# A third tile for loads of float64 weights in the first pass, its sums of weights all beside the gate matmuls, and the next pass's x scaled later

## The chip, the cores and the metric

The program runs on one core of one Trainium2 chip. The metric is the device time of one execution in microseconds (us); lower is better. TensorE (PE in the profile) multiplies, VectorE (DVE) and ScalarE (ACT) do elementwise work, SyncE (SP) issues nearly all DMAs, GpSimd (POOL) does a little at the start.

## What is computed

Attention on float32 inputs, followed by two feed-forward layers whose four weight matrices arrive as float64.

```
scores = cap * tanh((q @ k.T) / sqrt(64) / cap)          # 4 batches, 12 heads, 448 rows
x = softmax(scores) @ v                                  # -> 1792 x 768
h = x @ w_in;   g = h - tanh(h);              x = g @ w_out    # 768 -> 2048 -> 768
h = x @ w_in2;  g = h / (1 + exp(-1.702 h));  x = g @ w_out2
```

## The kernel before, in words

**Passes and stages.** Attention runs for all four batches first. Then two passes follow, each over two batches (896 rows). A pass has four stages: `gemm_in` of layer 0 (16 blocks of weights), `gemm_out` of layer 0 (16 blocks, in two halves of 8), `gemm_in` of layer 1, called the gate stage here (16 blocks), and `gemm_rows_seven`, the last product (seven sub-products of 4 blocks each, with half-size sums of the operands in the place of an eighth product). Every product is made of three float32r matmuls: high part by high part, high by low, low by high. So each block of weights must be split into `wh` (a cast on ACT, L76) and `wl` (a subtraction on DVE, L88). In the first three stages a block is 36 matmuls; in the last one 18, with 6 more in the first two sub-products for rows left over.

**Loads of doubles (first pass only).** A chunk of 768 KB of float64 weights is loaded by `dbl_dma` (L147) to a tile `wd`, of which there are two. `convert` makes float32 of it: ACT scales the upper word into a tile `wr` (`conv_exp`, L164; there are two of these too), DVE shifts and merges (L171, L177, L181). `conv_or` then stores the float32 chunk to DRAM (`single`, 384 KB) and issues the next `dbl_dma`, so that a load into a `wd` tile begins when that tile has been used up. A main chunk also gets its `wh` and `wl`. Besides the chunks that the stage itself needs, 16 chunks of the last stage's weights are converted ahead: the list `beside` (L140) says beside which blocks, 12 of them in `gemm_out` and 4 in the gate stage. `prepare` works two blocks ahead of PE (`LEAD`).

**Sums of weights.** The last stage needs sums of the quarters of its weight matrix. `sums_b` (L360) makes them in 8 pieces: four loads of 192 KB into tiles `gs`, four adds on DVE, four stores of 192 KB to DRAM tiles `t1` to `t4`. It is a generator that `ahead` advances once for each unit of `due`, and `rate` (set in `moe`, L1076) is what each block adds. A piece takes four steps; at a rate of 1.5 the 16 blocks of the gate stage give 24 steps, which is six pieces, and the other two follow at the start of the last stage.

**The next pass's x.** Attention results of batches 2 and 3 lie in DRAM without their softmax division. During the last stage of the first pass, twelve times, `x_load` (L1050) loads x and a row of reciprocals w into tiles tagged `far` and `t` (two of each), and `x_scale` multiplies them on DVE and splits the result (ACT cast, DVE subtraction). This is done at every second block from the first sub-product on, with one x loaded ahead. `rows_out` uses the same tags for output tiles.

**The last stage's right side.** `left` prepares the other operand for the next sub-product, sums of activation tiles (`add`, L306) and their split (`rl`, L88).

**Order.** After attention, a scheduler that has its own estimate of times places the instructions of each engine; each engine and the SP queue then works through its own list in order.

Of the kernel before, what the change touches and what calls it, by code (L numbers as in the profile page):

```python
# [9 lines left out]
F32 = mybir.dt.float32  # L10
F32R = mybir.dt.float32r
U32 = mybir.dt.uint32
# [25 lines left out]
def attention_moe_moe(ctx, tc, q, k, v, cap, w_in1, w_out1, w_in2, w_out2, out):  # L38
# [3 lines left out]
    P = 128  # L42
# [16 lines left out]
    def pool(name, bufs, **kw):  # L59
        return ctx.enter_context(tc.tile_pool(name=name, bufs=bufs, **kw))  # L60
# [76 lines left out]
    early = [0, 1, 2, 4, 6, 8, 10, 12, 14]  # L137
    A0, I0, R0 = KF, 2 * KF, 3 * KF
    KQ = KF // 4
    beside = [A0 + n for n in (2, 3, 4, 5, 6, 7, 10, 11, 12, 13, 14, 15)] + [I0 + n for n in (5, 8, 11, 14)]  # L140
    extra = {i: R0 + n % 4 * KQ + n // 4 for n, i in enumerate(beside)}
    order = early + [n for i in range(R0) if i not in early for n in (i, extra.get(i)) if n is not None]
    width = [(k1 - k0) * n for _, k0, k1, n in chunks]
# [4 lines left out]
    def dbl_dma():  # L148
        if n_dbl[0] < NCH:
            i = order[n_dbl[0]]  # L150
            src, k0, k1, n = chunks[i]
            t = wd_p.tile([P, WC, 2], U32, tag="wd", name="wd")
            for a in range(k0, k1, WG):
                z = min(k1, a + WG)
                nc.sync.dma_start(
                    out=t[:, (a - k0) * n:(z - k0) * n].rearrange("p (k f) w -> p k (f w)", f=n),
                    in_=src[a * P:z * P].rearrange("(k p) f -> p k f", p=P),
                )
            dbls[i] = t[:, :width[i]]
            n_dbl[0] += 1  # L160
# [472 lines left out]


    late = []

    def run_late():
        while late:
            late.pop(0)()
# [15 lines left out]
    def g_cubic(a, f, ps):  # L655
        n = a.stop - a.start
        t = g_p.tile([P, TC], F32, tag="t", name="g_t")[:, :n]
        far = g_p.tile([P, TC], F32, tag="far", name="g_far")[:, :n]
        th = nc.scalar.activation(out=t, in_=ps, func=AF.Tanh)
        df = nc.vector.tensor_tensor(out=far, in0=ps, in1=t, op=ALU.subtract)  # L660

        def rest():
            last = splits.pop(0) if splits else iter(())
            v = g1_p.tile([P, TC], F32, tag="v", name="g_v")[:, :n]
            if plain[0]:
                q = gr[f][:, a]
            else:
                q = g_p.tile([P, TC], F32, tag="q", name="g_q")[:, :n]
            m = g1_p.tile([P, TC], BF16, tag="m", name="g_m")[:, :n]
            nc.scalar.activation(out=v, in_=t, func=AF.Square)  # L670
            next(last, None)
            nc.scalar.activation(out=q, in_=v, func=AF.Square, scale=CUB_S, bias=cub_a)
            nc.scalar.activation(out=m, in_=v, func=AF.Relu, bias=cub_u)
            nc.vector.tensor_tensor(out=t, in0=v, in1=t, op=ALU.mult)
            next(last, None)
            nc.vector.scalar_tensor_tensor(out=q, in0=q, scalar=CUB_C, in1=t, op0=ALU.add, op1=ALU.mult)
            nc.vector.copy_predicated(out=q, mask=m.bitcast(U16), data=far)
            if not plain[0]:
                splits.append(g_split(a, f, q))
            for _ in last:  # L680
                pass
            if plain[0] and f < KH and a.stop == NT:
                right(0, f)

        def rest_behind():
            with tc.issue_after(th.ins), tc.issue_after(df.ins):
                rest()

        late.append(rest_behind)
        if f == KF - 1 and a.stop == NT and not plain[0]:  # L690
            late.append(lambda: list(splits.pop(0)))
# [89 lines left out]
    def gemm_out():  # L781
        for half in range(2):
            ps = [[ps_next("ps_y") for _ in range(3)] for _ in SPANS]
            for j in range(KF // 2):
                i, (wh, wl) = w_next()
                for (a0, a1), bank in zip(SPANS, ps):
                    for e in range(3):
                        c = slice(e * P, (e + 1) * P)
                        seq = [p for kk in range(2) for p in ((wh, gh, kk), (wh, gl, kk))]
                        seq += [(wl, gh, kk) for kk in range(2)]  # L790
                        for m, (w, x, kk) in enumerate(seq):
                            nc.tensor.matmul(  # L792
                                bank[e][:, :a1 - a0], w[:, kk, c], x[2 * j + kk][:, a0:a1],
                                start=(j == 0 and m == 0), stop=(j == KF // 2 - 1 and m == len(seq) - 1),
                            )
                        if e == 0:
                            (beside_it if a0 else ahead)(i)
                        if a0 == 0 and e == 1:
                            run_late()
                    if j == KF // 2 - 1:  # L800
                        for e in range(3):
                            x_out(3 * half + e, slice(a0, a1), bank[e][:, :a1 - a0])

    def gemm_out_seven():
# [1 line left out]
            return [ps_m.tile([P, 512], F32, tag="m", name="ps_y")[:, :S] for _ in range(3)]  # L806

        def temps(*tags):
            return [(g1_p if t == "v" else g_p).tile([P, TC], F32, tag=t, name="part")[:, :S] for t in tags]

        b11, b22 = ([gr[n + e][:, S:] for e in range(3)] for n in (2, 5))
        LO, HI = slice(0, S), slice(S, NT)
# [71 lines left out]
    def gemm_in_seven():  # L884
# [3 lines left out]
            return [(xh[3 * n + e][:, a], xl[3 * n + e][:, a]) for e in range(3)]  # L888

        def temp(tag):  # L890
            return (g1_p if tag == "v" else g_p).tile([P, TC], F32, tag=tag, name="part")[:, :S]

        right_of = {
            "11": part(0, LO), "12": part(1, LO), "s4": part(1, HI), "s1": part(0, HI),
# [47 lines left out]
    def gemm_rows_seven(b0):  # L942
        def three():
            return [ps_m.tile([P, 512], F32, tag="m", name="ps_o")[:, :HW] for _ in range(3)]

        def kept_sum(i):
            return sums[i // 2][:, i % 2 * HW:(i % 2 + 1) * HW]

# [19 lines left out]
        for p, name in enumerate(SEVEN_B):  # L968
            ps = three()
            for j in range(KQ):  # L970
# [19 lines left out]
                        left(SEVEN_B[p + 1], k)  # L990
                if p == 0 and j == 0:
                    run_late()
                if j % 2:
                    continue
                if loaded:
                    x_scale(*loaded.pop())
                if todo:
                    loaded.append((*todo[0], *x_load(b0 + NB, *todo.pop(0))))
            if p == 0 and side:
# [27 lines left out]
                rows_out(b0, 1, 6, rest[1])  # L1027

    def rows_out(b0, half, n, ps, plus=None, two=False):
        pool_n, tag = ((g_p, "q"), (g1_p, "v"), (g_p, "t"), (g_p, "far"))[n % 4]  # L1030
        o = pool_n.tile([P, TC], F32, tag=tag, name="o")[:, :HW]
        if plus is not None:
            nc.vector.scalar_tensor_tensor(
                out=o, in0=ps[:, :HW], scalar=0.5, in1=plus, op0=ALU.mult, op1=ALU.add
# [22 lines left out]
    def x_scale(s, i, x, w):  # L1057
        nc.vector.tensor_tensor(out=x, in0=x, in1=w, op=ALU.mult)
        x_split(s, i, x)

    def moe(b0):
        if b0 + NB == B:
            side.extend((sums_a(), sums_i()))
            rate[0] = 2.25
            yield from gemm_in(0)
            until("a")
            rate[0] = 0.5
            gemm_out_seven()
            until("i")
            gemm_in_seven()  # L1070
        else:
            yield from gemm_in(0)
            gemm_out()
            plain[0] = True
            open_plain()
            side.append(sums_b())  # L1076
            rate[0] = 1.5
            yield from gemm_in(1)
            rate[0] = 2.0
        gemm_rows_seven(b0)  # L1080

    wz = one_p.tile([P, 512], BF16, name="wz")
# [13 lines left out]
    pinned[0] = False  # L1096
    first.close()
    g_p = pool("g", 2)
    g1_p = pool("g1", 1)
    ps_m = pool("ps_m", 6, space=bass.MemoryType.PSUM)  # L1100
    g_stack = ExitStack()
    g_big = g_stack.enter_context(tc.tile_pool(name="g_big", bufs=1))
# [36 lines left out]
```

## Time and profile before

| | us |
|---|---|
| median of 3 runs (1117.69 to 1120.09) | 1120.02 |
| the profiled execution's own time | 1120.72 |
| its span, first to last instruction | 1118.9 |
| PE busy | 1087.7 (97%) |
| DVE busy | 930.9 (83%) |
| ACT busy | 667.7 (60%) |

PE is busy nearly all the time, so what can be gained lies in the few places where it waits. A matmul's record is longer than the step from its start to the next one's, so the time of a stage is judged against the time of the same number of matmuls in a stretch without waits. Sections of the span: attention to 200 us, `gemm_in` of the first pass to 320, `gemm_out` to 448.6, the gate stage to 566.0, the last stage to 685.7, and from there the second pass.

### The profile page before, as it was taken

The page shows a single profiled execution, that of the slowest core. Times are in us where ns is not written, and L with a number is a line of the kernel's source. Part 1 is how long each engine was busy: PE and PEld are TensorE (multiplying, and loading weights), DVE is VectorE, ACT ScalarE, POOL GpSimd, SP SyncE. Part 2 cuts the span into 40 slices and gives each one's busy share as a digit, 9 for nine tenths or more (in the row PEclk, how much of TensorE's full clock was granted, in tenths as well). Part 3 has the DMA queues.
Part 4 walks back from the last instruction along what each step waited for, and adds up shares of the span by engine and source line. Part 5 has one row for each costly group of instructions (what it writes and reads, how often), then busy time and mean ns, then how long its engine had stood idle before and what let it go on. Part 6 is the DMA issues. An engine that isn't in the chain of part 4 may idle for free.

```text
span 1118.9 us, 16125 instructions
## 1 busy us (share of the span) xinstructions
PE 1087.7 (97%) x5579; PEld 888.8 (79%) x5579; DVE 930.9 (83%) x1467; ACT 667.7 (60%) x1022; POOL 59.0 (5%) x56
## 2 busy tenths in 40 slices
PE   9999998999999898999989999999999999999998
PEld 3333332789898787899979898888999999999997
DVE  4788999789996666988799784989999898889674
ACT  6898887899872322544325553776755554455452
POOL 0013344100000000000000000000000000000000
PEclk9999999999999999999999999999999999999999
DMA  6776686454537688899955748888655333333445
GB/s 143 201 205 182 194 241 206 159 198 141 185 121 261 249 258 270 266 303 296 299 181 171 215 145 281 295 292 297 203 171 195 115 99 115 112 106 106 127 133 151
DMA packets 156466, 220.58 MB, mean 197 GB/s; under 512 B 58672, under 2 KB 108640, under 8 KB 156384
## 3 DMA queue, kind: packets, MB, share of 16 engines
q1 hardware_dynamic: 155088, 218.94, 62.0%
q8 instruction: 44, 0.72, 0.3%
q10 hardware_dynamic: 1296, 0.61, 0.2%
q14 instruction: 38, 0.31, 0.1%
HBM read 160.83 MB, written 58.68 MB: 196 GB/s over the span
## 4 chain that ended last, share of the span: by engine, by line
PE 61%; DMA 15%; DVE 13%; ACT 6%; issue 4%; SPq 2%; ACTq 0%; DVEq 0%
PE ps_h L767 16%; PE ps_y L825 9%; PE ps_h L909 9%; PE ps_o L979 9%; PE ps_pv L491 7%; DMA wd<-in_moe_w_out_dram 6%; PE ps_sc L450 5%; DMA wd<-in_moe_w_in_dram 3%; DMA whole<-t 2%; DVE wd L171 2%; DVE wr L181 2%; ACT wr L164 2%; PE ps_o L964 2%; DVE wl L88 2%; DVE gs L306 1%
## 5 line engine op out<-in xcount | busy, mean ns | idle before, releaser
L767 PE MATMUL ps_h<-xh,wh 128*128 128x384 f32 (+1 forms) x576 | 209.6, 364 | 2.8 <-ACT wh L76 1.8
L767 PE MATMUL ps_h<-xl,wh 128*128 128x384 f32 (+1 forms) x576 | 210.4, 365 | 0.7 <-DVE xl L88 0.7
L76 ACT CAST wh<-whole 128x768 fp32r<-128x768 f32 (+1 forms) x124 | 100.9, 813 | 90.7 <-PE ps_h L909 35.7
L88 DVE TENSOR_TENSOR wl<-whole,wh 128x768 fp32r<-128x768 f32 (+1 forms) x124 | 115.2, 930 | 26.7 <-ACT wh L76 25.4
L767 PE MATMUL ps_h<-xh,wl 128*128 128x384 f32 (+1 forms) x576 | 131.1, 362 | 0.0
L979 PE MATMUL ps_o<-wl,rh 128*128 128x384 f32 x336 | 114.3, 340 | 9.3 <-DVE wl L88 9.2
L767 PEld LDWEIGHTS ps_h<-xh,wh 128*128 128x128 f32 x576 | 108.1, 188 | 16.3 <-ACT wh L76 2.1
L767 PEld LDWEIGHTS ps_h<-xl,wh 128*128 128x128 f32 x576 | 108.1, 188 | 13.3 <-DVE xl L88 1.2
L767 PEld LDWEIGHTS ps_h<-xh,wl 128*128 128x128 f32 x576 | 104.6, 188 | 12.5 <-issue 1.4
L979 PE MATMUL ps_o<-wh,rh 128*128 128x384 f32 x336 | 113.2, 337 | 1.2 <-ACT wh L76 1.0
L979 PE MATMUL ps_o<-wh,rl 128*128 128x384 f32 x336 | 112.9, 336 | 0.0
L76 ACT CAST rh<-gr 128x384 fp32r<-128x384 f32 (+1 forms) x141 | 72.8, 527 | 62.3 <-PE ps_y L825 26.7
L164 ACT ACTIVATE wr<-wd 128x768 f32<-128x768 f32 x64 | 57.7, 903 | 71.5 <-DMA wd<-in_moe_w_out_dram 43.8
L171 DVE TENSOR_SCALAR wd<-wd 128x768 uint16<-128x768 uint16 x57 | 59.7, 1048 | 40.3 <-ACT wr L164 40.3
L88 DVE TENSOR_TENSOR rl<-gr,rh 128x384 fp32r<-128x384 f32 (+1 forms) x141 | 80.0, 577 | 7.4 <-ACT rh L76 6.9
L469 ACT ACTIVATE t<-ps_sc,tsc 128x896 f32<-128x896 f32 x72 | 69.9, 1005 | 26.7 <-PE ps_sc L450 26.6
L792 PE MATMUL ps_y<-gh,wh 128*128 128x512 f32 (+1 forms) x192 | 71.0, 370 | 6.9 <-ACT wh L76 6.9
L979 PEld LDWEIGHTS ps_o<-wl,rh 128*128 128x128 f32 x336 | 63.4, 189 | 12.8 <-DVE wl L88 12.8
L471 ACT ACTIVATE t<-t,cpos 128x896 f32<-128x896 f32 x72 | 72.3, 1041 | 0.4
L792 PE MATMUL ps_y<-gl,wh 128*128 128x512 f32 (+1 forms) x192 | 70.3, 366 | 0.0
L450 PE MATMUL ps_sc<-qk 64*128 64x448 f32 x288 | 68.4, 573 | 0.8 <-ACT qk L76 0.6
L491 PE MATMUL ps_pv<-t,rv 128*64 128x448 f32 x288 | 64.0, 550 | 3.9 <-ACT t L469 3.4
(143 smaller groups left out, 2280.9 us busy)
## 6 DMA issues: line engine op xcount, KB each, us to landing
wd<-in_moe_w_in_dram SPq DMA_DIRECT2D x64, 384.0 KB
wd<-in_moe_w_out_dram SPq DMA_DIRECT2D x32, 768.0 KB
whole<-single SPq DMA_DIRECT2D x51, 384.0 KB
single<-wr SPq DMA_DIRECT2D x48, 384.0 KB
whole<-t SPq DMA_DIRECT2D x32, 384.0 KB
pair<-single SPq DMA_DIRECT2D x32, 384.0 KB
s<-pair SPq DMA_DIRECT2D x32, 384.0 KB
whole<-s SPq DMA_DIRECT2D x32, 384.0 KB
```

Of the source, the lines that this page charges most:

```text
L76: pin(nc.scalar.copy(out=dst, in_=src))
L88: pin(nc.vector.tensor_tensor(out=dst, in0=src, in1=hi.bitcast(F32), op=ALU.subtract))
L164: pin(nc.scalar.mul(out=raws[i][:, :width[i]], in_=dbls[i][:, :, 1].bitcast(F32), mul=2.0 ** -112))
L171: pin(nc.vector.tensor_scalar(out=half[:, :, 2], in0=half[:, :, 1], scalar1=F64_LOW, scalar2=None, op0=ALU.mult))
L450: pin(nc.tensor.matmul(ps[:, j, :S], qk[a, kc], qk[a, :S], start=True, stop=True))
L471: ins = pin(nc.scalar.activation(out=tt[g, c], in_=tt[g, c], func=AF.Exp, scale=cpos))
L491: pin(nc.tensor.matmul(ps[a, :S], w, t[:, j], start=(c == 0), stop=(c == KC - 1)))
L767: pin(nc.tensor.matmul(ps, w[:, kk, :], x[kk][:, a], start=(m == 0), stop=(m == len(seq) - 1)))
L792: nc.tensor.matmul(bank[e][:, :a1 - a0], w[:, kk, c], x[2 * j + kk][:, a0:a1], start=(j == 0 and m == 0), stop=(j == KF // 2 - 1 and m == ...
L825: nc.tensor.matmul(ps[e], w[:, kk, c], x, start=(k == 0 and m == 0), stop=(k == KH - 1 and m == 2))
L909: nc.tensor.matmul(ps, w, x, start=(m == 0), stop=(m == len(seq) - 1))
L979: nc.tensor.matmul(ps[n], x[:, t], w[:, kk, :], start=(k == 0 and m == 0), stop=(k == KH - 1 and m == 2),)
```

## The change

Four things are edited.

1. The tiles `q` (two) and `v`, `m` (one each) move from the pools `g` and `g1` to pools of their own that can be closed (`swap_pools`). After the first block of `gemm_out` in the first pass they are closed, one more `wd` tile is opened in their place and one more `dbl_dma` is issued. From then on every third load of doubles goes to the new tile. At the start of `gemm_rows_seven` the tiles are swapped back.
2. The last four chunks converted beside others are moved from gate blocks 5, 8, 11, 14 to gate blocks 3, 5, 7, 9.
3. The rate of `sums_b` in the gate stage is 2.0 and not 1.5.
4. `x_load` and `x_scale` begin in the third sub-product; there are two x loaded ahead and not one; and from the fifth sub-product on they come at every block.

```diff
-    beside = [...] + [I0 + n for n in (5, 8, 11, 14)]
+    beside = [...] + [I0 + n for n in (3, 5, 7, 9)]
@@ dbl_dma
-            t = wd_p.tile([P, WC, 2], U32, tag="wd", name="wd")
+            more = some.get("wd") if n_dbl[0] % 3 == 0 else None
+            t = (more or wd_p).tile([P, WC, 2], U32, tag="wd", name="wd")
@@ beside run_late
+    some = {}
+    def temp_p(tag):
+        return some.get(tag, g_p)
+    def swap_pools(**kinds):
+        if "stack" in some:
+            some.pop("stack").close()
+        some.clear()
+        some["stack"] = ExitStack()
+        for name, bufs in kinds.items():
+            some[name] = some["stack"].enter_context(tc.tile_pool(name=f"some_{name}", bufs=bufs, side="right"))
+    def open_temps():
+        swap_pools(q=2, v=1)
@@ gemm_out
                         if a0 == 0 and e == 1:
                             run_late()
+                            if half == j == 0:
+                                swap_pools(wd=1)
+                                dbl_dma()
@@ gemm_rows_seven
+        if "wd" in some:
+            open_temps()
...
-                if j % 2:
+                if p < 2 or (p + j) % 2 and p < 4:
                     continue
-                if loaded:
-                    x_scale(*loaded.pop())
+                if len(loaded) > 1 or loaded and not todo:
+                    x_scale(*loaded.pop(0))
                 if todo:
                     loaded.append((*todo[0], *x_load(b0 + NB, *todo.pop(0))))
@@ moe
             side.append(sums_b())
-            rate[0] = 1.5
+            rate[0] = 2.0
             yield from gemm_in(1)
-            rate[0] = 2.0
         gemm_rows_seven(b0)
```

No instruction is added or removed on any engine. PE's order is the same. What moves, moves on DVE, ACT and SP between the start of `gemm_out` and the end of the first pass.

At the start of `gemm_out`, on SP. `single` are stores of converted chunks, `wd` the loads of doubles. Before:

```order
L185 DMA single32_218<-wr_3369 128x768
L155 DMA wd_3375<-in_moe2_w_out_dram 128x2x768
L185 DMA single3_189<-wr_3395 128x768
L155 DMA wd_3401<-in_moe_w_out_dram 128x2x768
L185 DMA single36_222<-wr_3425 128x768
```

and now:

```order
L186 DMA single32_218<-wr_3379 128x768
L156 DMA wd_3365<-in_moe2_w_out_dram 128x2x768
L156 DMA wd_3385<-in_moe_w_out_dram 128x2x768
L186 DMA single3_189<-wr_3405 128x768
L156 DMA wd_3411<-in_moe2_w_out_dram 128x2x768
```

One more load is issued there, and every later load stands one store earlier in the queue.

At the entry to the last stage, on DVE: from the `wl` of the stage's first block to that of its second (`whole` is a block loaded from DRAM, `gs` a tile of sums, `gr` a tile of activations, `restl` the low part of left-over rows). Before:

```order
L88 TENSOR_TENSOR wl_5242<-whole_5183,wh_5241 128x768
L699 SCALAR_TENSOR_TENSOR gr13_4248<-g_t_5236,ps_h_5217 128x384
L306 TENSOR_TENSOR gs0_4251<-gr0_4235,gr8_4243 128x384
L88 TENSOR_TENSOR restl13_4302<-gr13_4248,resth13_4301 128x128
L306 TENSOR_TENSOR gs7_4258<-gs7_4258,gs6_4257 128x384
L306 TENSOR_TENSOR gs0_4251<-gs0_4251,gr0_4235 128x384
L306 TENSOR_TENSOR gs6_4257<-gs6_4257,gs4_4255 128x384
L306 TENSOR_TENSOR gs1_4252<-gr1_4236,gr9_4244 128x384
...
L88 TENSOR_TENSOR wl_5294<-whole_5245,wh_5293 128x768
```

and now:

```order
L88 TENSOR_TENSOR wl_5270<-whole_5213,wh_5269 128x768
L715 SCALAR_TENSOR_TENSOR gr13_4258<-g_t_5264,ps_h_5245 128x384
L307 TENSOR_TENSOR gr3_4248<-gr3_4248,gr11_4256 128x384
L88 TENSOR_TENSOR restl13_4312<-gr13_4258,resth13_4311 128x128
...
L88 TENSOR_TENSOR wl_5326<-whole_5273,wh_5325 128x768
```

There were 14 instructions between the two and there are 9. From the first `wl` to the fourth there were 37 besides these and there are 25: adds of the last pieces of sums and x are gone from there, and adds of `left` for later sub-products now stand before the first `wl`.

In the first two sub-products, on SP (`w` and `x` are the next pass's). Before:

```order
L252 DMA whole_5362<-single35_221 128x768
L527 DMA w_5399<-wrow2_112 64x448 x2
L252 DMA whole_5407<-single36_222 128x768
L527 DMA w_5487<-wrow2_112 64x448 x2
L527 DMA w_5583<-wrow2_112 64x448 x2
L1053 DMA x_5582<-xd2_2_100 128x448
L252 DMA whole_5449<-single37_223 128x768
```

and now:

```order
L253 DMA whole_5401<-single35_221 128x768
L253 DMA whole_5437<-single36_222 128x768
L253 DMA whole_5471<-single37_223 128x768
L253 DMA whole_5505<-single38_224 128x768
L253 DMA whole_5545<-single39_225 128x768
```

The loads of x and w now stand among the blocks of the fourth to sixth sub-products (ten of x and all twelve pairs of w there; before, six of x and eight pairs of w stood among those of the fourth and fifth).

## Rows read from the trace of the kernel before

**Rows 1.** What TensorE waited for; columns: us in total, times, longest.

```profile
PE ps_o L979 <- DVE wl L88: 9.2, 9, 3.3
PE ps_y L792 <- ACT wh L76: 6.9, 5, 2.5
```

**Rows 2.** Busy time by stage, 320 to 686 us; (x) counts instructions.

```profile
core 0: us, PE busy (x) PEld busy (x) DVE busy (x) ACT busy (x) POOL busy (x), PEclk, DMA share, GB/s
320.10:382.80 62.70, 59.22 (x291) 52.06 (x289) 43.40 (x60) 22.99 (x32) 0.00 (x0) 1.00 0.66 228
382.80:448.60 65.80, 60.83 (x288) 52.84 (x288) 44.26 (x57) 21.82 (x30) 0.00 (x0) 0.98 0.79 258
448.60:507.00 58.40, 57.42 (x282) 51.13 (x283) 50.68 (x81) 28.70 (x50) 0.00 (x0) 1.00 0.88 285
507.00:566.00 59.00, 59.00 (x295) 53.05 (x294) 46.84 (x77) 22.35 (x40) 0.00 (x0) 1.00 0.93 303
566.00:590.10 24.10, 19.17 (x98) 17.95 (x97) 23.63 (x49) 8.78 (x18) 0.00 (x0) 0.93 0.49 151
590.10:624.60 34.50, 34.50 (x200) 34.33 (x199) 29.05 (x53) 18.46 (x35) 0.00 (x0) 1.00 0.59 176
624.60:656.80 32.20, 28.59 (x158) 26.84 (x157) 27.70 (x48) 18.41 (x33) 0.00 (x0) 1.00 0.64 194
656.80:685.70 28.90, 27.45 (x153) 26.04 (x151) 18.10 (x31) 10.44 (x17) 0.00 (x0) 1.00 0.61 184
```

**Rows 3.** Chain of work, second pass: start us, us, what.

```profile
685.95 116.50 PE ps_h L767 x576
...
1059.86 12.48 PE ps_o L979 x72
```

**Rows 4.** Chain of work in the first half of gemm_out.

```profile
342.61 1.04 DVE wd L171
...
345.48 4.97 DMA wd<-in_moe_w_out_dram
...
369.51 1.04 DVE wd L171
...
372.37 6.28 DMA wd<-in_moe_w_out_dram
```

**Rows 5.** What ScalarE waited for, 322 to 450 us.

```profile
ACT wr L164 <- DMA wd<-in_moe_w_out_dram: 41.6, 17, 3.9
```

**Rows 6.** TensorE in order of time: first stall of gemm_out, its cause in brackets.

```profile
372.90 0.50 PE L792 MATMUL ps_y<-gh,wh 128*128 128x512 f32 x1 [1.22 <-ACT wh L76]
```

**Rows 7.** DMA issues of the whole run.

```profile
wd<-in_moe_w_out_dram SPq DMA_DIRECT2D x32, 768.0 KB
...
single<-wr SPq DMA_DIRECT2D x48, 384.0 KB
...
gs<-single SPq DMA_DIRECT2D x32, 192.0 KB
```

**Rows 8.** Chain of work in the gate stage: a store of a chunk.

```profile
546.28 4.17 DMA single<-wr
```

**Rows 9.** VectorE in order of time at the entry to the last stage.

```profile
565.19 0.95 DVE L88 TENSOR_TENSOR wl<-whole,wh 128x768 fp32r<-128x768 f32 x1
...
572.56 0.56 DVE L306 TENSOR_TENSOR gs<-gs,gr 128x384 f32<-128x384 f32 x1
573.03 0.95 DVE L88 TENSOR_TENSOR wl<-whole,wh 128x768 fp32r<-128x768 f32 x1
573.90 0.55 DVE L699 SCALAR_TENSOR_TENSOR gr<-g_t,ps_h 128x384 f32<-128x384 f32 x1
...
585.26 0.96 DVE L88 TENSOR_TENSOR wl<-whole,wh 128x768 fp32r<-128x768 f32 x1
```

**Rows 10.** What the SP queue waited for, 566 to 686 us.

```profile
SPq L252 <- DVE wl L88: 43.5, 26, 3.7
SPq L1053 <- DVE xl L88: 7.5, 7, 2.3
```

More of the change, by code (lines that the diff above doesn't have):

```diff
@@ L139, in attention_moe_moe @@
     KQ = KF // 4
-    beside = [A0 + n for n in (2, 3, 4, 5, 6, 7, 10, 11, 12, 13, 14, 15)] + [I0 + n for n in (5, 8, 11, 14)]
+    beside = [A0 + n for n in (2, 3, 4, 5, 6, 7, 10, 11, 12, 13, 14, 15)] + [I0 + n for n in (3, 5, 7, 9)]
     extra = {i: R0 + n % 4 * KQ + n // 4 for n, i in enumerate(beside)}
@@ L663, in rest @@
             last = splits.pop(0) if splits else iter(())
-            v = g1_p.tile([P, TC], F32, tag="v", name="g_v")[:, :n]
+            v = temp_p("v").tile([P, TC], F32, tag="v", name="g_v")[:, :n]
             if plain[0]:
@@ L667, in rest @@
             else:
-                q = g_p.tile([P, TC], F32, tag="q", name="g_q")[:, :n]
-            m = g1_p.tile([P, TC], BF16, tag="m", name="g_m")[:, :n]
+                q = temp_p("q").tile([P, TC], F32, tag="q", name="g_q")[:, :n]
+            m = temp_p("v").tile([P, TC], BF16, tag="m", name="g_m")[:, :n]
             nc.scalar.activation(out=v, in_=t, func=AF.Square)
@@ L808, in temps @@
         def temps(*tags):
-            return [(g1_p if t == "v" else g_p).tile([P, TC], F32, tag=t, name="part")[:, :S] for t in tags]
+            return [temp_p(t).tile([P, TC], F32, tag=t, name="part")[:, :S] for t in tags]
         b11, b22 = ([gr[n + e][:, S:] for e in range(3)] for n in (2, 5))
@@ L890, in temp @@
         def temp(tag):
-            return (g1_p if tag == "v" else g_p).tile([P, TC], F32, tag=tag, name="part")[:, :S]
+            return temp_p(tag).tile([P, TC], F32, tag=tag, name="part")[:, :S]
         right_of = {
@@ L1029, in rows_out @@
     def rows_out(b0, half, n, ps, plus=None, two=False):
-        pool_n, tag = ((g_p, "q"), (g1_p, "v"), (g_p, "t"), (g_p, "far"))[n % 4]
-        o = pool_n.tile([P, TC], F32, tag=tag, name="o")[:, :HW]
+        tag = ("q", "v", "t", "far")[n % 4]
+        o = temp_p(tag).tile([P, TC], F32, tag=tag, name="o")[:, :HW]
         if plus is not None:
@@ L1098, in attention_moe_moe @@
     g_p = pool("g", 2)
-    g1_p = pool("g1", 1)
+    open_temps()
+    ctx.callback(lambda: some.pop("stack").close())
     ps_m = pool("ps_m", 6, space=bass.MemoryType.PSUM)
```

## The prediction

> **What bounds the kernel now.** I read first what TensorE waits for. After attention nearly all of it is two kinds of wait, for the high part of a weight block in `gemm_out` and for the low part in the last stage [rows 1]. Then I cut the first pass into its stages [rows 2] and judged each by the pace of a stretch without waits [rows 3]: 576 matmuls in 116.5 us (16 blocks of 7.28 us) and 72 in 12.48 us (0.1733 us each) in the last stage. What each stage loses: the two halves of `gemm_out` take 62.7 and 65.8 us where 58.25 would do, 4.45 and 7.55 lost; the gate stage 117.4 for 116.5, 0.9 lost; the first sub-product of the last stage, 96 matmuls, 24.1 for 16.6, 7.5 lost; the next two (198) 34.5 for 34.3, 0.2; the fourth and fifth (156) 32.2 for 27.0, 5.2; the last two (150) 28.9 for 26.0, 2.9. Together 28.7 us. No change of order can win more than that.
>
> Part of it is the clock: it is 0.98 of 2.4 GHz in the second half of `gemm_out` and 0.93 in the first sub-product [rows 2], 1.3 and 1.7 us, after stalls of 2.5 and 3.3 us [rows 1]. Where those stalls go, this goes.
>
> **Why `gemm_out` waits.** The chain goes round one load tile: a load, the scaling on ScalarE, three steps on VectorE, the issue of the next load. From the shift at 342.61 to that at 369.51 are three rounds [rows 4], 8.97 us each, of which the load is 5.0 to 6.3. Two tiles give two chunks a round; a block with a chunk beside it needs two, so it costs 8.97 us where TensorE takes 7.28, and ScalarE stands 41.6 us waiting for loads [rows 5]. Six blocks of each half have such a chunk, which makes 6 x 1.69 = 10.1 us short in a half; the first half lost 4.45, so the lead of two blocks swallowed 5.7. That is why the first stall comes only at 372.9, 52 us into the stage [rows 6].
>
> **The third tile.** Three chunks in a round of 8.97 us would make 6.0 us for two. The round will grow, as three loads share the DMA engines; it may reach 10.9 us, a load of 7.2, before a block costs more than 7.28. The bytes: two loads of 768 KB and two stores of 384 KB [rows 7] are 2.36 MB a block, 324 GB/s at TensorE's pace. The trace of before shows no stage of the first pass above 303 [rows 2]; at that rate a block costs 7.79, 0.51 too much, 3.1 us in a half, which the lead of 5.7 swallows. At the 258 of the stage as it is, nothing would be won; a loss is excluded as long as a round serves three chunks and not two. So the gain lies between 0 and 12.0 us; it is nearest to the upper end, because the DMA share of 0.66 and 0.79 shows idle time between loads and not full engines. I keep 1.0 us of loss: **11.0 won**. The one extra load needs `q`, `v` and `m` of the stage before to be finished, and SP waits for that; it stands behind a store that waits for VectorE anyway, so I cost it at nothing; if VectorE is late there, at part of one load, which the lead covers.
>
> **The gate stage.** Here the change adds. A main chunk moves 768 + 384 KB a block; the four chunks beside others now fall into the first eight blocks, half a chunk a block, 576 KB; the sums at rate 2.0 do a piece in two blocks, four loads and four stores of 192 KB [rows 7], 768 KB a block. That is 2496 KB or 2.56 MB a block, 351 GB/s at TensorE's pace, in eight blocks. The stage ran at 285 and 303 GB/s with a share of 0.88 and 0.93 [rows 2], so it is nearly full: at 303 a block costs 8.4 us, 1.2 short, 9.3 us over eight blocks. Against that stands a lead of two blocks, up to 14.6 us, of which 5.7 were usable in `gemm_out` and which is larger at the entry now, since `gemm_out` ends without a deficit. Scaled to a share of 1.0 the rate would be 303 / 0.93 = 326, an estimate: 7.85 us a block, 4.6 short. Loss between 0 and 9.3 - 5.7 = 3.6, nearest to the estimate: I take 1.5 in the place of 0.9, **0.6 lost**. The second eight blocks move 1.97 MB, 270 GB/s, and recover. The Trainium skill (DMA: Bandwidth & Descriptors, Specifications) gives a core about 358 GB/s of HBM; by that the eight blocks would take 7.1 us each, the gate stage would lose nothing, and the total would be 0.6 us better. The trace, with 303 at a share of 0.93, does not bear that out, and I go by the trace.
>
> **The entry to the last stage.** VectorE is the bound there: 23.63 busy of 24.1 [rows 2]. From the `wl` of the first block to that of the fourth it needed 20.1 us, without idle time [rows 9]; TensorE takes three blocks of 24 matmuls, 12.5 us, in that time. The difference, 7.6, is the loss of 7.5. Between these two `wl` stood 37 other instructions and now stand 25; at steps of 0.47 us (572.56 to 573.03) and 0.87 for each of three `wl` (573.03 to 573.90) [rows 9] that is 11.8 + 2.6 = 14.4, still 1.9 above TensorE. If VectorE comes with a lead, nothing is lost, if not 1.9, or up to 4 if it comes later than now, for 8 us of adds now stand ahead of the first `wl`. I take 1.0: **6.5 won**. SP is relieved too: eight blocks follow each other without an x between.
>
> **The later x.** The fourth and fifth sub-product lost 5.2 us with six x and eight pairs of w among their loads: SP waited 7.5 us in seven waits for the tiles of x, with weight blocks behind it, and 43.5 for weight tiles [rows 10]. Now ten x and twelve pairs stand there and in the sixth, and each load needs the tile of the x that is scaled in the same step, where before there was a step between. Lower bound: nothing lost, 5.2 won; upper: 5.2 x 10 / 6 = 8.7 and the 2.9 of the end doubled, 6.4 lost. Nearest is the same density over one more sub-product: 6.6 in the place of 5.2, **1.4 lost**; the 2.9 of the last two stay.
>
> **Sum.** 11.0 - 0.6 + 6.5 - 1.4 = 15.5 us. The profiled execution took 1120.7, which would become 1105.2; the median of the runs shown is 0.7 below it, 1120.0, which gives **1104.5 us**.
>
> **Rivals.**
> *Stores bind `gemm_out`.* There are still two `wr` tiles. One is held from its scaling until its store has landed: about 3.5 us of the round's engine steps (8.97 less a load of 5.0 and the issues) and a store of 4.17 [rows 8], 7.7 for two chunks on two tiles, 0.4 above 7.28. With longer stores, 5.5 us, it is 9.0 as before and the third tile is idle. Against it: what ScalarE waits for before a scaling is the load [rows 5]. Then 1104.5 + 11 = 1115.5. Chance 0.13.
> *x runs into the weights.* The upper bound above: 6.4 in the place of 1.4 lost, some of it in output tiles that share tags with x: 1109.5 to 1112. For it: SP's waits [rows 10]. Chance 0.18.
> *The gate stage becomes the bound: slower.* The eight blocks of 2.56 MB fall behind faster than the lead holds. To eat the 16.1 us won elsewhere and the 0.9 lost here already they would have to fall 17.0 + 5.7 = 22.7 behind, 2.84 a block: 10.1 us, or 253 GB/s. From there it decides, and `gemm_out` ran at 258 [rows 2]. At 240 (10.7 a block, 27.1 behind, 21.4 lost) it is 1124.4. For it: SP takes its list in order, and loads of doubles now stand behind sums that wait for VectorE. Against: 303 GB/s in the same mix. Chance 0.09.
> *Nearly all goes.* The later x costs nothing (6.6 better) and the entry is free (1.0): 1104.5 - 7.6 = 1096.9. For it: what x delays is only what SP holds back [rows 10], and SP's list is freer now. Chance 0.15.
>
> **How the numbers follow.** My forecast, 1101 to 1108, has 0.45. The likeliest time stays 1104.5. The range leaves out the slow rival and the stores with x on top, and takes in the rest: from 1095 (all but 3.7 of the 28.7 won) to 1116. A measurement of this kernel can tell about 0.2%, 2.2 us. Slower: the gate rival, 0.09. Within 0.2%: of the 0.13 of the stores 0.05 with the loss by x on top, 1115.5 + 5. Faster: the rest, 0.86.
>
> **What would show it.** Right: TensorE's wait for `wh` in `gemm_out` falls from 6.9 us to under 2, its halves to 58 to 59 us at a DMA rate near 310; ScalarE's wait for loads falls below 15; the clock stays at 1.00; the first sub-product takes 17 to 19 us. Wrong: halves above 62 us with ScalarE waiting for stores; a gate stage above 120 us with a DMA share of 0.95; the fourth to sixth sub-product losing more than 9 us with SP waiting for `xl`.

## The result and the profile after

The changed kernel takes **1105.6 us** (median of 4 runs, 1104.4 to 1107.1) beside 1118.9 of the kernel before (median of 4 runs, 1116.9 to 1120.1): a ratio of **0.988, 95% interval 0.986 to 0.991**, 13 us less. Its profiled execution took 1106.7 with a span of 1104.8, against 1120.7 with a span of 1118.9. The forecast was 1104.5.

The stages of the changed kernel, cut as those of before [rows 2]; the columns are the same (stretch and its length; busy time and count of PE, PEld, DVE, ACT, POOL; clock, DMA share, GB/s):

```profile
320.06:378.20 58.14, 58.14 (x290) 52.20 (x289) 43.24 (x61) 23.21 (x33) 0.00 (x0) 1.00 0.78 267
378.20:441.33 63.13, 59.99 (x290) 53.62 (x289) 49.06 (x65) 23.83 (x33) 0.00 (x0) 0.97 0.88 298
441.33:500.00 58.67, 57.61 (x284) 50.95 (x283) 51.72 (x83) 26.99 (x49) 0.00 (x0) 1.00 0.93 304
500.00:559.22 59.22, 59.22 (x296) 53.27 (x295) 53.20 (x95) 22.35 (x42) 0.00 (x0) 1.00 0.75 253
559.22:575.86 16.64, 16.64 (x98) 16.64 (x97) 16.33 (x32) 8.81 (x18) 0.00 (x0) 1.00 0.28 85
575.86:610.18 34.32, 34.32 (x200) 34.32 (x199) 23.19 (x38) 16.96 (x30) 0.00 (x0) 1.00 0.58 169
610.18:640.09 29.91, 27.86 (x158) 26.97 (x157) 26.64 (x48) 17.58 (x32) 0.00 (x0) 1.00 0.71 212
640.09:669.97 29.88, 28.02 (x153) 25.89 (x151) 20.82 (x35) 12.53 (x22) 0.00 (x0) 1.00 0.69 209
```

The first half of `gemm_out` takes 58.1 us in place of 62.7: PE is busy all the time. The second half takes 63.1 in place of 65.8, at a clock of 0.97: it still loses 4.9. The gate stage takes 117.9 in place of 117.4. The first sub-product of the last stage takes 16.64, exactly its ideal, in place of 24.1. The last four take 59.8 in place of 61.1. The second pass begins at 669.97 and not at 685.7, 15.7 us earlier. Of these 14.1 are left in the span, because the second pass itself is 1.6 longer (last section).

What PE waited for most after attention (us in total, times, longest):

```profile
PE ps_o L1001 <- DVE wl L88: 4.0, 7, 1.2
PE ps_y L808 <- DVE xl L88: 3.1, 1, 3.1
PE ps_h L783 <- DVE xl L88: 1.1, 2, 0.7
```

The wait for `wh` in `gemm_out` (6.9 us before, [rows 1]) is gone. In its place stands one wait of 3.1 us in `gemm_out` that the trace of before does not have, for `xl`: a PSUM bank that VectorE has not emptied yet. In order of time it is this matmul, 6 us into the second half, after a wait that begins 3 us into it:

```profile
384.50 0.50 PE L808 MATMUL ps_y<-gh,wh 128*128 128x512 f32 x1 [3.14 <-DVE xl L88]
```

A half keeps six banks, and the program has eight (`ps_s` and `ps_m`). The second half starts on the two free ones; its third needs a bank that holds the first half's result until ScalarE has cast it to `xh` and VectorE has made `xl`. ScalarE at that time:

```profile
376.94 0.84 ACT L76 CAST wh<-wr 128x768 fp32r<-128x768 f32 x1 [2.54 <-DVE wr L182]
377.68 0.91 ACT L165 ACTIVATE wr<-wd 128x768 f32<-128x768 f32 x1
381.19 0.83 ACT L76 CAST wh<-wr 128x768 fp32r<-128x768 f32 x1 [2.60 <-DVE wr L182]
381.92 0.90 ACT L165 ACTIVATE wr<-wd 128x768 f32<-128x768 f32 x1
382.73 1.54 ACT L76 CAST xh<-ps_y 128x512 fp32r<-128x512 f32 x3
```

PE had finished the three banks that these casts read by 375.5. But in ScalarE's list the casts of x stand behind a cast of the next weight block, which waits 2.60 us for VectorE, and a scaling. The Trainium skill (PSUM — Partial Sum Buffer, Engine vs sequencer instructions) says that ScalarE's and VectorE's queues are strictly first in, first out; these rows agree, with 2.6 us of ScalarE idle in front of casts that could have run.

And ScalarE's waits over 322 to 450 us:

```profile
ACT wr L165 <- DMA single<-wr: 33.5, 13, 4.6
ACT wh L76 <- DVE wr L182: 19.1, 8, 3.2
...
ACT wr L165 <- DMA wd<-in_moe_w_out_dram: 3.7, 1, 3.7
```

It hardly waits for loads any more (3.7 us; 41.6 before, [rows 5]), but 33.5 us for stores to leave the two `wr` tiles.

### The profile page after: what moved, and what is told of

It reads as the page before. It is cut to its first block, busy times and chain, and to the rows that moved or that the text cites. A ratio compares the mean times of both kernels' runs of the same rounds, so it can differ in the third digit from the quotient of the medians.

```text
span 1104.8 us, 16127 instructions
## 1 busy us (share of the span) xinstructions
PE 1085.7 (98%) x5579; PEld 888.4 (80%) x5579; DVE 932.2 (84%) x1467; ACT 668.5 (61%) x1022; POOL 59.1 (5%) x56
## 3 DMA queue, kind: packets, MB, share of 16 engines
q1 hardware_dynamic: 155088, 218.94, 62.2%
## 4 chain that ended last, share of the span: by engine, by line
PE 74%; DMA 9%; DVE 8%; ACT 4%; issue 4%; SPq 0%; ACTq 0%; DVEq 0%
PE ps_h L783 29%; PE ps_y L844 9%; PE ps_h L928 9%; PE ps_o L1001 8%; PE ps_pv L492 7%; PE ps_sc L451 5%; DMA whole<-t 4%; DMA single<-wr 3%; PE ps_o L986 2%; DVE wl L88 2%; DVE wr L182 1%; DVE wd L172 1%; ACT wh L76 1%; PE ps_qk L430 1%; ACT wr L165 1%
## 5 line engine op out<-in xcount | busy, mean ns | idle before, releaser
L76 ACT CAST rh<-gr 128x384 fp32r<-128x384 f32 (+1 forms) x141 | 73.6, 528 | 85.9 <-PE ps_o L1001 35.2
L783 PEld LDWEIGHTS ps_h<-xl,wh 128*128 128x128 f32 x576 | 108.1, 188 | 14.1 <-DVE xl L88 1.9
L783 PEld LDWEIGHTS ps_h<-xh,wl 128*128 128x128 f32 x576 | 104.6, 188 | 12.5 <-issue 1.4
L470 ACT ACTIVATE t<-ps_sc,tsc 128x896 f32<-128x896 f32 x72 | 69.9, 1006 | 26.6 <-PE ps_sc L451 26.6
L172 DVE TENSOR_SCALAR wd<-wd 128x768 uint16<-128x768 uint16 x57 | 59.6, 1046 | 26.9 <-ACT wr L165 26.6
L1001 PEld LDWEIGHTS ps_o<-wl,rh 128*128 128x128 f32 x336 | 63.1, 188 | 6.3 <-DVE wl L88 6.2
```

The lines of the kernel that those rows point to most:

```text
L76: pin(nc.scalar.copy(out=dst, in_=src))
L172: pin(nc.vector.tensor_scalar(out=half[:, :, 2], in0=half[:, :, 1], scalar1=F64_LOW, scalar2=None, op0=ALU.mult))
L470: pin(nc.scalar.activation(out=t, in_=ps[:, :, :S], func=AF.Tanh, scale=tsc))
L783: pin(nc.tensor.matmul(ps, w[:, kk, :], x[kk][:, a], start=(m == 0), stop=(m == len(seq) - 1)))
L1001: nc.tensor.matmul(ps[n], x[:, t], w[:, kk, :], start=(k == 0 and m == 0), stop=(k == KH - 1 and m == 2),)
```

## The experiments

Two quantities differ by 2 to 3 us from one execution to the next, whatever the kernel: the end of attention (197.4 to 200.2 us in the profiles) and the gate stage of the second pass (102.2 or 104.2). So whole times are compared by ratios over several runs, and profiles by the length of a stage. Lengths in us, from the same cut as above:

| kernel | median us | ratio to before, interval | gemm_out | gate | 1st | 2nd, 3rd | last four |
|---|---|---|---|---|---|---|---|
| before | 1119 to 1120 | 1 | 62.7 + 65.8 | 117.4 | 24.1 | 34.5 | 61.1 |
| the change | 1105.6 | 0.988 (0.986 to 0.991) | 58.1 + 63.1 | 117.9 | 16.6 | 34.3 | 59.8 |
| e1 pools moved only | 1120.4 | 1.000 (0.999 to 1.002) | 62.9 + 65.2 | 117.4 | 25.1 | 34.5 | 59.9 |
| e2 third tile only | 1104.5 | 0.987 (0.984 to 0.990) | 58.1 + 63.1 | 120.5 | 16.8 | 35.2 | 58.2 |
| e3 change without tile | 1115.3 | 0.997 (0.995 to 0.998) | 63.3 + 65.8 | 120.2 | 20.7 | 34.3 | 60.1 |
| e4 change, x as before | 1102.2 | 0.984 (0.982 to 0.987) | 58.1 + 61.0 | 117.3 | 16.6 | 34.8 | 56.7 |
| e5 third `wr` tile | 1101.8 | 0.984 (0.980 to 0.987) | 58.1 + 61.3 | 116.3 | 16.6 | 34.3 | 59.5 |
| e6 e5 with x as before | 1099.6 | 0.982 (0.979 to 0.985) | 58.1 + 61.3 | 116.3 | 16.6 | 34.3 | 57.3 |
| e7 change, sums as before | 1103.3 | 0.986 (0.982 to 0.990) | 58.2 + 62.2 | 118.5 | 16.6 | 34.3 | 60.6 |
| e8 change, x spread | 1102.4 | 0.984 (0.981 to 0.987) | 58.1 + 64.0 | 116.8 | 16.6 | 34.3 | 56.2 |
| e9 casts of x first | 1100.5 | 0.983 (0.981 to 0.986) | 58.1 + 59.8 | 116.3 | 16.6 | 34.3 | 59.7 |
| e10 e6 with casts of x first | 1099.9 | 0.983 (0.981 to 0.985) | 58.1 + 61.0 | 116.3 | 16.6 | 34.7 | 58.8 |
| e11 e10 with x spread | 1099.6 | 0.982 (0.979 to 0.985) | 58.1 + 63.9 | 116.3 | 16.6 | 34.3 | 57.2 |
| e12 the change again | 1105.2 | 0.989 (0.986 to 0.991) | 58.1 + 63.7 | 118.1 | 16.6 | 34.3 | 61.8 |

Ideals by the pace without waits [rows 3]: 58.25 + 58.25, 116.5, 16.6, 34.3, 53.0.

The table has one profile of each kernel. Through `gemm_out` the change, e2, e4, e7, e8 and e12 have the same lists on ScalarE and VectorE, and the second half still takes 61.0 to 64.0 us among them, with a wait of 2.5 to 3.6 for the bank. A difference within that spread tells nothing.

### e1: the pools alone

The change with these lines and what reads them taken out, and with edits 2, 3 and 4 undone:

```diff
-                            if half == j == 0:
-                                swap_pools(wd=1)
-                                dbl_dma()
```

> The kernel before, only with q, v and m in pools at the other end of the memory; no third load tile, sums and x as before. Theory 'placement costs nothing': within 0.2% of before, 1119 us. Rival 'the new addresses slow the gate stage of the second pass', which took 102.1 us before and 104.2 in the changed kernel: that stage is at 104.2 here too and the whole is 2 us slower than before, 1121.

Measured: no difference (0.9985 to 1.0021). The second pass's gate stage took 104.2 here, but in e12, which is the changed kernel once more, 102.2. So the length of that stage does not come with the addresses: both lengths occur with the same ones.

### e2 and e3: the third tile alone, and everything but the tile

e2 undoes edits 2, 3 and 4; e3 undoes the three lines above with what reads them.

> The third load tile alone; sums and x as before. Theory 'a load tile bound gemm_out until half-way, then a PSUM bank does': the first half falls from 62.7 to 58 us, the second from 65.8 to 63 with a wait of about 3 us for xl near its start, the entry to the last stage still loses 7.5; 1119 - 7 = 1112. Rival 'the two tiles wr and their stores bind gemm_out': halves stay above 62, no gain, 1118 or more.

> The changed kernel without the third load tile. If the parts add up: it loses the 7 us of gemm_out, 1105.6 + 7 = 1112.6, with the entry to the last stage still free. Rival 'the gate stage lives on the lead that gemm_out hands it': gemm_out now ends with no lead, the eight blocks full of sums lose up to 5 us more, and the time is 1115 to 1118.

The tile alone gives all that the change gives: 0.987. `gemm_out` did what was expected, 58.1 and 63.1. What was not expected is the entry to the last stage, which now loses 0.1 us and not 7.5, with the sums where they were before:

```profile
377.92:441.04 63.12, 60.01 (x290) 53.58 (x289) 47.13 (x63) 23.14 (x31) 0.00 (x0) 0.97 0.87 296
441.04:561.58 120.54, 118.69 (x578) 105.45 (x577) 102.99 (x174) 49.87 (x90) 0.00 (x0) 0.99 0.83 274
561.58:578.34 16.76, 16.76 (x98) 16.61 (x97) 16.73 (x35) 6.88 (x14) 0.00 (x0) 1.00 0.42 128
```

The reason is in the lead. VectorE's `wl` of the gate stage's last block, and of the last stage's first, in e2:

```profile
546.96 0.96 DVE L88 TENSOR_TENSOR wl<-wr,wh 128x768 fp32r<-128x768 f32 x1
...
555.74 0.95 DVE L88 TENSOR_TENSOR wl<-whole,wh 128x768 fp32r<-128x768 f32 x1
```

PE begins these blocks at 554.55 and 561.81, 6.6 and 5.1 us after the `wl` are done. Before, the first of the two:

```profile
557.32 0.95 DVE L88 TENSOR_TENSOR wl<-wr,wh 128x768 fp32r<-128x768 f32 x1
```

The block began at 558.96, 0.7 us later; and the last stage's first `wl` ended at 566.14 [rows 9], 0.1 us before its block began. The first matmul of the last stage, in e2 and before:

```profile
561.81 0.33 PE L1001 MATMUL ps_o<-wh,rh 128*128 128x384 f32 x1
```

```profile
566.23 0.33 PE L979 MATMUL ps_o<-wh,rh 128*128 128x384 f32 x1
```

VectorE entered the last stage with its adds still in front of it. The lead is older than the gate stage. The `wl` of the gate stage's first block and that block's first matmul, in e2 and before:

```profile
436.63 0.95 DVE L88 TENSOR_TENSOR wl<-wr,wh 128x768 fp32r<-128x768 f32 x1
441.27 0.39 PE L783 MATMUL ps_h<-xh,wh 128*128 128x512 f32 x1
```

```profile
448.82 0.96 DVE L88 TENSOR_TENSOR wl<-wr,wh 128x768 fp32r<-128x768 f32 x1 [0.30 <-ACT wh L76]
448.84 0.50 PE L767 MATMUL ps_h<-xh,wh 128*128 128x512 f32 x1 [1.83 <-ACT wh L76]
```

In e2 this `wl` is done 3.7 us ahead of its block, before it was 0.9 late: 4.6 us apart, where the last stage's first blocks are 5.0 apart. So `gemm_out` and the entry did not have a loss each: both were one missing lead, and a third tile gives it back for both. Two things limit this. The tile stays open through the gate stage, where ScalarE waited 10.7 us for loads before and not at all in e2, and no run closes it earlier. And the gate stage of e2 is 3.1 us longer than before, which leaves 4.3 of the 7.4 us won at the entry; in e7, below, it is 1.1 longer and 6.4 of 7.5 are left. The gate stage of e2 loses 4.0 us, nearly all at its start, in waits for the `xl` that the second half of `gemm_out` leaves, and at a low clock after them (0.91 in its first 7 us).

Without the tile (e3) the edits together win 3.8 us by the ratio. The gate stage has no lead to start from and waits for weights more than before (4.2 us, 1.8 before), as the rival said (PE's waits, 447 to 568 us):

```profile
PE ps_h L782 <- ACT wh L76: 4.2, 3, 1.9
```

and the entry still loses 4.1. The parts do not add: 14.5 us for the tile alone and 3.8 for the rest would be 18.3; together they are 13.

### e4, e8: where the x stand

```diff
-                if p < 2 or (p + j) % 2 and p < 4:
+                if j % 2:
...
-                if len(loaded) > 1 or loaded and not todo:
-                    x_scale(*loaded.pop(0))
+                if loaded:
+                    x_scale(*loaded.pop())
```

> The changed kernel with the x scheduled as before (one in two blocks from the first sub-product on, each scaled a step later). Theory 'the adds of the sums held VectorE at the entry': the first sub-product loses at most 2 us (18.6 at most) and the fourth and fifth lose their 5 again in place of 2.9; 1105.6 + 2 + 2 = 1109.6 at most, 1107 likeliest. Rival 'x and w in SP's and VectorE's list held the entry': the first sub-product loses 4 or more, 20.6 and up; 1110 or more.

e4 is faster than the change, 0.984 (0.982 to 0.987) against 0.988 and 0.989, though the intervals touch; 1107 us was expected and 1102.2 measured. The first sub-product is free with the x among its blocks, so x did not hold the entry. The fourth and fifth, and the last two, take 28.3 and 28.4 us in place of 29.9 and 29.9:

```profile
605.65:633.94 28.29, 27.32 (x158) 27.00 (x157) 25.16 (x44) 17.16 (x31) 0.00 (x0) 1.00 0.63 193
633.94:662.33 28.39, 27.35 (x153) 26.01 (x151) 17.40 (x30) 10.49 (x17) 0.00 (x0) 1.00 0.60 184
```

VectorE is busy 25.2 and 17.4 us there, against 26.6 and 20.8 in the change, and what SP waited for in the last stage fell from

```profile
SPq L253 <- DVE wl L88: 52.1, 25, 4.8
```

to

```profile
SPq L253 <- DVE wl L88: 38.4, 24, 4.8
```

So edit 4 by itself costs 3.1 us in this profile. The 2.1 us by which the second half of `gemm_out` is shorter lie within the spread named above. e8 spreads the x instead:

```diff
-                if p < 2 or (p + j) % 2 and p < 4:
+                if p < 1 or (p + j) % 2 and p < 6:
```

> The changed kernel with the x spread: from the second sub-product on, one in two blocks, up to the sixth. Theory 'what the later x costs is weight blocks that stand behind x and its w on SP in the last four sub-products': these lose 6.75 us together in the changed kernel and 4 here; 1103. Rival 'the losses there are those of the tail of each sub-product whatever x does': 6.75 again, 1105.6.

The last four take 56.2, 3.1 above the ideal, where 4 was expected:

```profile
610.13:638.91 28.78, 27.61 (x158) 26.98 (x157) 25.02 (x44) 17.16 (x31) 0.00 (x0) 1.00 0.63 189
638.91:666.31 27.40, 26.82 (x152) 25.93 (x151) 16.50 (x29) 10.47 (x17) 0.00 (x0) 1.00 0.61 185
```

By its ratio e8 is the equal of e4. Kernels with the later x take 59.5 to 61.8 in these four (the change, e3, e5, e7, e9, e12); with the third tile and x as before or spread, 56.2 to 58.8 (e2, e4, e6, e8, e10, e11).

### e7: the sums as before

Edits 2 and 3 undone.

> The changed kernel with the sums and the four chunks beside the gate stage placed and paced as before; third load tile and later x stay. Theory 'one missing lead was the loss of gemm_out and of the entry both, and the tile alone gives it back': first sub-product still loses under 1 us, 1105 to 1108. Rival 'the sums free the entry': it loses 4 or more, 1109 and up.

The first sub-product loses nothing. The time is 0.986 (0.982 to 0.990), not to be told from the change. With a third tile, where the sums stand makes no difference that shows. Whether they are worth something without a tile was tried only together with the x (e3).

### e5, e6: a third wr tile

In the room that the closed pools leave beside the third `wd` tile, closed again at the end of `gemm_out`:

```diff
...
+                                wr_stack = ExitStack()
+                                some["wr"] = wr_stack.enter_context(tc.tile_pool(name="some_wr", bufs=1, side="right"))
...
+        n_raw[0] += 1
-        raws[i] = wr_p.tile([P, WC], F32, tag="wr", name="wr")
+        raws[i] = (some.get("wr") if n_raw[0] % 3 == 0 and "wr" in some else wr_p).tile([P, WC], F32, tag="wr", name="wr")
```

> The changed kernel with a third wr tile during gemm_out (in the room that the idle temporaries leave). Theory 'two wr tiles, each held until its store has landed, make ScalarE late, and with it the draining of the PSUM banks half-way': ScalarE's wait for stores in gemm_out falls from 33.5 us to under 10, TensorE's wait of 3.1 us at the start of the second half to under 1, that half loses 1.5 at most in place of 4.9; 1105.6 - 3.5 = 1102. Rival 'the DMA engines are full there': ScalarE waits for loads instead, the stall stays, 1105 to 1106.

> The same with the x scheduled as before. If the two gains add: 1102.2, which was measured with x as before, less 2 to 3.5 for the second half of gemm_out, 1099 to 1100, the lowest of all. Rival 'x as before won only through the second half of gemm_out, which happened to lose 2.8 there and not 4.9': no difference to the third wr tile with the later x, 1102.

ScalarE no longer waits for stores; it waits for loads again. e5 over 322 to 441 us:

```profile
ACT wr L167 <- DMA wd<-in_moe_w_out_dram: 33.3, 15, 4.3
ACT wh L76 <- DVE wr L184: 17.2, 7, 2.6
```

The second half takes 61.3 us at 319 GB/s, and the gate stage loses nothing: its waits for `xl` are gone. But PE still waits 2.4 us for the bank, where under 1 was expected, and the half loses 3.1 where 1.5 at most was expected. Neither can be told from e4, with two `wr` tiles (2.5 us, and a half of 61.0). So what a third `wr` tile does for this wait is not shown; it leaves the casts of x behind the weight's. The time, 1101.8, is what was expected. e6 adds the x as before: 1099.6, inside the 1099 to 1100 expected, but not to be told from e5 by the intervals.

### e9, e10, e11: the casts of x first

In the last block of a half, the next block's cast to `wh` is issued behind the three casts of x (`behind_x` holds these):

```diff
-                        if e == 0:
+                        if e == 0 and (a0 or j < KF // 2 - 1):
                             (beside_it if a0 else ahead)(i)
...
                             x_out(3 * half + e, slice(a0, a1), bank[e][:, :a1 - a0])
+                        if a0 == 0:
+                            ahead(i)
...
-        conv_hi(i)
+        with ExitStack() as st:
+            for ins in behind_x:
+                st.enter_context(tc.issue_after(ins))
+            conv_hi(i)
```

> The changed kernel with one order turned round: in the last block of a half of gemm_out the cast of the next weight block is issued behind the three casts of x that free the PSUM banks. Theory 'the wait of 3.1 us half-way is those casts of x standing behind a weight's cast, which waits 2.6 us for VectorE': the wait falls under 1 and the second half loses 2 at most in place of 4.9, 1103. Rival 'it is the two wr tiles': a scaling that waits for a store still stands ahead of them, the wait stays near 3, 1105 to 1106.

This alone, with two `wr` tiles, takes the second half to 59.8 us, within 1.6 of its ideal, and the gate stage to 116.3:

```profile
375.65:435.47 59.82, 58.44 (x290) 52.12 (x289) 48.79 (x66) 25.04 (x36) 0.00 (x0) 1.00 0.92 307
435.47:551.73 116.26, 116.26 (x578) 104.37 (x577) 104.83 (x180) 48.44 (x86) 0.00 (x0) 1.00 0.85 284
```

PE's wait is 1.4 us (under 1 was expected). The three casts run before the weight's:

```profile
374.80 0.91 ACT L165 ACTIVATE wr<-wd 128x768 f32<-128x768 f32 x1
376.95 0.93 ACT L165 ACTIVATE wr<-wd 128x768 f32<-128x768 f32 x1 [1.24 <-DMA single<-wr]
377.78 1.54 ACT L798 CAST xh<-ps_y 128x512 fp32r<-128x512 f32 x3
379.20 0.85 ACT L76 CAST wh<-wr 128x768 fp32r<-128x768 f32 x1
```

ScalarE waits for stores in `gemm_out` no less than in the change, 40.9 us in all (39.7 in e12). The wait and the half lie outside the spread of the change's list, so the wait goes with the order of ScalarE's list, and a third `wr` tile is not needed to shorten it. The time is 1100.5, 0.983 (0.981 to 0.986), below the change's (0.986 to 0.991, twice).

> Third wr tile, x as before, and that order turned round. By either theory on the bank the wait is gone: second half within 1 us of the ideal 58.25, 3 less than with the third wr tile alone (which still waited 2.4 there), 1099.6 - 2.5 = 1097. If the weight block behind is late instead: a wait for wh or wl some 5 us later, 1099 to 1100.

> The same with the x spread from the second to the sixth sub-product in place of as before. The last stage lost 4.2 us with x as before and 3.1 with x spread: 1 us less than the run beside it, 1096; or no difference that can be told, 1097.

These two miss: 1097 and 1096 to 1097 were expected. The wait for the bank is 2.2 us in e10 and 3.9 in e11, the second half takes 61.0 and 63.9. ScalarE in e10:

```profile
379.43 0.89 ACT L167 ACTIVATE wr<-wd 128x768 f32<-128x768 f32 x1 [3.27 <-DMA wd<-in_moe_w_out_dram]
380.22 1.06 ACT L800 CAST xh<-ps_y 128x512 fp32r<-128x512 f32 x2
382.32 0.90 ACT L167 ACTIVATE wr<-wd 128x768 f32<-128x768 f32 x1 [1.03 <-DMA wd<-in_moe_w_out_dram]
```

The scaling ahead of the casts now waits 3.27 us for its load, where the one in e9 waited 1.24 for a store, and another scaling stands among the casts. Holding only the weight's cast behind x is not enough there; holding the scalings behind as well was not tried. Both are still the equals of e6 and e9 by their ratios, e11 through the spread x. The versions whose intervals lie below those of both kernels are e6, e9, e10 and e11, at 1099.6 to 1100.5; among them the runs do not tell.

### e12: the change again

> The changed kernel itself, beside the others on the same chip: 0.988 of before, as measured, 1105 to 1106.

0.9887 (0.9863 to 0.9912), as the first time.

## Why the prediction was right, and where

The time was 1.1 us from the forecast, but the terms of its sum were not, and that they came out to it is luck. In the two profiles the third tile won 3.8 us less than forecast and the second pass was 1.6 longer, which no term held; the entry (1.0), the x (2.7) and the stages beside them (0.3) came out better.

**The third tile, 11.0 won: mis-sized in one way, misplaced in another.** In `gemm_out` it won 7.2 us (4.6 in the first half, 2.6 in the second), since 4.8 are still lost where I kept 1.0; in e12 it was 6.6. The step that failed is "I keep 1.0 us of loss": I looked at the DMA engines for what is late next, and they held (the halves reached 267 and 298 GB/s, and the second 319 in e5). Next was the draining of PSUM banks half-way. Before, PE stood for `wh` at the first matmul of the second half, twelve matmuls ahead of that place, and no wait for the bank shows behind it:

```profile
383.08 0.80 PE L792 MATMUL ps_y<-gh,wh 128*128 128x512 f32 x1 [2.54 <-ACT wh L76]
```

The trace of before could not show the wait, but the code did: six banks of eight in use, and the casts of x in ScalarE's list behind weights. The Trainium skill (Perfetto Trace Analysis, Matmuls under Optimizing Tensor Performance) asks that groups of matmuls rotate through different banks, so that emptying one overlaps the next group. Here two free banks stand for six, and that costs 3.1 us in this trace; e9 has the same banks, and 1.4.

**The entry, 6.5 won: the size right (7.5), the cause not.** I counted 37 instructions between two `wl`, 25 in the change, and priced the difference. The price per instruction was right, and the lead was left out. The traces give both (times in us, the lead read as in e2 above):

| | before | e3 | e2 | e7 | the change |
|---|---|---|---|---|---|
| instructions from the first `wl` to the fourth | 37 | 36 | 33 | 33 | 25 |
| VectorE's time from the one to the other | 20.1 | 18.9 | 17.7 | 17.8 | 14.7 |
| more than PE's 12.5 | 7.6 | 6.4 | 5.2 | 5.3 | 2.2 |
| lead of the first `wl` on its block | 0.1 | 3.3 | 5.1 | 5.4 | 3.8 |
| lost by the first sub-product | 7.5 | 4.1 | 0.1 | 0.0 | 0.0 |

The loss is what VectorE needs more than PE, less its lead, but for 1.0 us in e3 (at a clock of 0.92), which this leaves open. So the lead of the tile covers the 33 instructions of the sums as before (e2, e7), and edits 2 and 3 win nothing at the entry beside it. "If VectorE comes with a lead, nothing is lost" stands in that part of the prediction; but I did not ask what the tile does to that lead. The step that failed is the sum, which adds two terms that were one.

**The gate stage, 0.6 lost: 0.5 measured, but not by the DMA engines.** Its first half moved 304 GB/s at a share of 0.93 (285 and 0.88 before), and PE waited for no weight in it. What is lost are two waits for `xl` at its start, 1.1 us. These are again x drained late, and they are gone in e5 and e9 (116.3). In e9 the same half moves 325 GB/s without a wait of PE, so the 303 that I went by was not the most the engines give:

```profile
435.46:494.06 58.60, 58.60 (x292) 52.62 (x291) 54.05 (x87) 28.18 (x48) 0.00 (x0) 1.00 0.96 325
```

By the 358 GB/s of the Trainium skill (DMA: Bandwidth & Descriptors, Specifications) the stage would have lost nothing. It lost nothing by loads, and no stage here shows such a rate.

**The later x, 1.4 lost: the sign right only against the right neighbour.** Against the kernel before, the last four sub-products became 1.3 us shorter in the first profile and 0.7 longer in e12. Against the same kernel with x as before (e4) they are 3.1 longer. I scaled the loss of before, which is larger than that of the same x with the tile: with the tile and the old x the four lose 3.6 to 5.7 (e2, e4, e6, e10), without the tile 8.1 and 6.9 (before, e1). That the missing lead swelled it fits, but no run shows it apart. Nor does the 6.6 of that term follow from its rows: 5.2 over three sub-products in place of two is 7.8.

**The rivals.** That stores bind `gemm_out` is half true: ScalarE's wait went over from loads to stores, 33.5 us, as that rival said; but the lead covers it, and e9 comes to 59.8 us with the same two tiles. x did not run into the weights to the full price of the upper bound. The gate stage did become short of weights, but only where it was given no lead (e3), and there the kernel was still faster than before. Of "nearly all goes" the free entry came true, the later x at no cost did not.

**The signs given.** Right: the wait for `wh` under 2 us (none), ScalarE's wait for loads under 15 (3.7), the first half at 58 to 59 us. The first sub-product came out better than the 17 to 19 given. Not so: the halves ran at 267 and 298 GB/s and not near 310. A sign of being wrong, "halves above 62 us with ScalarE waiting for stores" did appear, in the second half, and the clock there was 0.97.

## What to carry to other kernels

When stages follow each other with a lead between them, a loss in a later stage can be the lead that an earlier one did not hand on. Before adding two such losses, look how late each producer is at the boundary, price the first repair with the second left out, and take the lead that it hands on off the price of the second. And when a wait goes, ask of the same matmul what it waits for next: PSUM banks in reuse show no wait as long as something else is later.

## What the runs showed that was not expected

**The step of a 448-column matmul has two lengths.** The second pass's gate stage in the kernel before, in the change, and in the change again:

```profile
906.34:1008.48 102.14, 102.14 (x505) 94.67 (x505) 89.53 (x159) 53.16 (x96) 0.00 (x0) 1.00 0.38 113
```

```profile
890.69:994.85 104.16, 104.16 (x505) 94.59 (x505) 89.97 (x161) 53.40 (x96) 0.00 (x0) 1.00 0.36 110
```

```profile
891.10:993.30 102.20, 102.20 (x506) 94.58 (x505) 89.75 (x161) 53.24 (x96) 0.00 (x0) 1.00 0.37 112
```

PE is busy throughout at a clock of 1.00, with the same 504 matmuls (505 or 506 by the cut), and yet a step is 0.2027 or 0.2067 us. In eight of the fourteen profiles the step falls from the longer to the shorter one 98 to 110 us after the beginning of the stage before, and then stays; in the other six it never does. In seven of the eight it falls right behind a short pause, 98 us into that stage, where the weight load of a matmul waits for `wl`; here in the kernel before:

```profile
900.39 0.19 PEld L825 LDWEIGHTS ps_y<-rh,wl 128*128 128x128 f32 x1 [0.36 <-DVE wl L88]
```

But all fourteen have this pause, at the same matmul, and in the other seven the step stays. Both happen with the same program. The profile of the change was one of the six and that of before one of the eight: 2.0 us against the change that have nothing to do with it. What decides whether it changes stays open.

**The same stall does or does not cost the clock.** The 3 us behind the wait half-way through `gemm_out`, in e12 (a wait of 3.57 us) and in e7 (3.55):

```profile
382.40:385.40 3.00, 2.75 (x7) 2.17 (x8) 3.00 (x6) 2.36 (x6) 0.00 (x0) 0.57 0.44 171
```

```profile
382.50:385.50 3.00, 2.80 (x13) 2.39 (x14) 3.00 (x6) 2.48 (x5) 0.00 (x0) 1.00 0.43 168
```

In e12 the granted clock is 0.57, most of the stretch at 1.2 GHz, and 7 matmuls begin; in e7 it is 1.00, 2.4 GHz, and 13 begin. PE had been busy without a wait through the first half in both. The second half lost 5.4 us in e12 and 3.9 in e7. The prediction set the clock's share to the stalls; a stall's length alone does not tell whether it comes.
